# A delta rule followed by a two-layer network: where the rescaling of keys, the masks, the big loads and two steps of the first product stand in the prologue

## The chip, the cores and the metric

The kernel runs on one core of one Trainium2 chip. The metric is the device time of one execution in microseconds (us). The engines are TensorE (PE, matrix products), VectorE (DVE), ScalarE (ACT), GpSimd (POOL) and SyncE (SP, which issues transfers). Each engine takes its instructions in the order of the program, and semaphores hold it until its operands are ready.

## The reference

```python
B, H, S, D = 4, 8, 768, 48
k_n = k / (norm(k) + 1e-6)
state = zeros(B, H, D, D)
for t in range(S):
    y[:, :, t] = einsum('bhd,bhde->bhe', q[:, :, t], state)
    v_old = einsum('bhde,bhd->bhe', state, k_n[:, :, t])
    state += beta[:, :, t] * outer(k_n[:, :, t], v[:, :, t] - v_old)
x = y.transpose(0, 2, 1, 3).reshape(3072, 384)
h = x @ w_in                      # 384 x 2048, given in 64-bit floats
g = h / (1 + exp(-1.702 * h))
out = g @ w_out                   # 2048 x 384, given in 64-bit floats
```

## The kernel before

The sequence of 768 steps is cut into chunks of C = 128, so there are 24 units (6 chunks, 4 batches of 8 heads). Within a chunk the recurrence becomes a triangular system: Gram products of the keys (gram), the inverses of its 32 x 32 diagonal blocks (invert, worked by DVE for 128 blocks at once) and a chain of block solves, called hops (together): PE multiplies, ACT copies the result to SBUF, and the next hop needs the copy. The first four units are whole chunks of one batch each (Step); the later ones are taken as halves (Half). The output of two units forms a tile xT of 256 rows, for which hidden computes gelu(x @ w_in) in 16 steps of two, each of three f32 products of 128 x 256 (ph); the second product is po.

The weights come as 64-bit floats, and DVE turns them into 32-bit floats in six instructions a piece, one of them a clamp on ACT (conversion, line 265). Pieces overlap each other (conversions, 318): the first four are halves of the first two quarters of w_in (128 x 768 words), then six thirds of the other quarters (128 x 512), then the 16 blocks of w_out (128 x 384, two pairs as one). After the first eight blocks the second inverse is worked (invert(1)), then the other eight. All this is one stream called behind. fill(us) (393) records as much of it as us of its own cost estimates, at least one instruction, wherever the program stands; the order on DVE is thus written by hand, by where fill stands and what it is given. A finished piece starts loads of later blocks of raw weights (fetch_in, 236; fetch_out, 253), which go into places that are free by then.

Ahead of the steady part (slot, from unit 3 on, with PE full) stands a prologue:

- keys of units 0 to 3 are loaded, normalized and turned, the first inverse is worked, and the Gram products of these units are made;
- the squares of the keys of units 4 to 7 (the second keys) are summed; roots_second (478) lets POOL take the power, and DVE then rescales the keys;
- the first hops, eight passes of the loop at line 1508 for units 0 and 1. Among them stand warm matmuls (of no use but to keep PE busy), the turning of the second keys by PE (turn, in passes 2 to 5), the masks (select, a POOL instruction of 128 x 1024 for each unit) and the thirds of w_in. paced (1473) lets POOL copy one word of a finished result into the place that a load is to fill, so that the load starts behind that result;
- put_out for units 0 and 1: outputs and states, and ACT copies them to xT;
- the loads of the first three blocks of w_out, of bL (beta for the later inverses, 16 small transfers) and of keys and queries, most of them issued by POOL (other_queue);
- the later hops, the loop at line 1568 for units 2 and 3. Each pass makes a Gram product of the second keys (passes 0 to 2), a step of hidden (feed, 1561) and a fill;
- a loop of 25 passes (1612) with a fill and a feed each, in which the keys of units 8 to 11 are prepared (prepare_early, 1597): ACT squares them, DVE sums, POOL takes the power, DVE adds and inverts (rn), ACT scales the keys in eight instructions, PE turns them (psT), and so on, one step each two passes. Also the scores psQ of unit 4 stand there, in pass 18;
- the first half of po for units 0 and 1 (both_written, 1260), and then slot after slot.

Of the kernel before, what the change touches and what calls it, by code (L numbers as in the profile page):

```python
# [18 lines left out]
def kernel(  # L19
# [28 lines left out]
    KC = DM // 128  # L48
# [3 lines left out]
    HB = 2  # L52
# [84 lines left out]
    def pinned(op):  # L137

        return lambda *a, **kw: tc.keep_in_program_order(op(*a, **kw))  # L139
# [12 lines left out]
    sync, beside = pinned(nc.sync.dma_start), pinned(nc.scalar.dma_start)  # L152
# [30 lines left out]
    def warm(n, after=None):  # L183
        ps = ps_moe.tile([128, 2, 256], F32, tag="moe", name="ps_warm")
        if after is not None:
            after(ps[:, 0, 0:1], 0.0)
        twice = ones.rearrange("p (o k) -> p o k", o=1).broadcast_to([128, 2, 256])
        for _ in range(n // 2):
            pe.matmul(ps, lhsT=ones[:, 0:128], rhs=twice, start=True, stop=True)
        if n % 2:  # L190
            pe.matmul(ps[:, 0], lhsT=ones[:, 0:128], rhs=ones, start=True, stop=True)
# [11 lines left out]
    def as_raw(words, shape):  # L203
        a, b = shape
        return words.rearrange("p (j n o) -> p j n o", j=a, n=b)

    def as_rows(raw):
        return raw.bitcast(moe_w_in.dtype).rearrange("p j n o -> p j (n o)")
# [13 lines left out]
    def quarter(i):  # L222
        size = KC * NQ * 2
        at = 1 if i == 1 else 0
        return as_raw(raws[:, at * size : (at + 1) * size], (KC, NQ))

    def place_thirds():

        for j in range(KC):
            words = g_tile().rearrange("p f t -> p (f t)").bitcast(I32)  # L230
            thirds.append(as_raw(words, (1, NQ)))
        for a in (3072, 2048):
            thirds.append(as_raw(TW[:, a : a + 2 * NQ].bitcast(I32), (1, NQ)))
        thirds.append(as_raw(raws[:, 4 * NQ : 6 * NQ], (1, NQ)))

    def fetch_in(i, other=None, js=None, only=None):

        f = slice(i * NQ, (i + 1) * NQ)
        for j in range(KC) if js is None else js:
            dst = as_rows(thirds[(i - 2) * KC + j])[:, 0] if i >= 2 else as_rows(quarter(i))[:, j]  # L240
            for p, r, m, step in x_rows:
                if only is not None and p // DP != only:
                    continue
                (other if other and (p >= DP or js) else sync)(
                    out=dst[p : p + m], in_=moe_w_in[r + j * step : r + j * step + m, f]
                )
# [6 lines left out]
    def fetch_out(f, dma=sync):  # L253

        if f in outside:
            slot = outside[f]
            if slot not in slots:
                slots[slot] = wk.tile([128, 2 * DM], I32, tag=slot[:2].strip("2"), name="raw", bufs=4 if slot[0] == "M" else 3)
            words = slots[slot]
        else:  # L260
            words = raws[:, inside[f] * DM : (inside[f] + 2) * DM]
        places[f] = as_raw(words, (1, DM))
        dma(out=as_rows(places[f])[:, 0], in_=moe_w_out[f * 128 : (f + 1) * 128, :])
# [129 lines left out]
    def fill(us):  # L393
        while us > 0:
            us -= next(behind, us)
# [82 lines left out]
    def roots_second(areas):  # L478

        z, r = (TW[:, a : a + B * H].rearrange("p (b h) -> p b h", b=B) for a in (1792, 1856))  # L480
        for o in range(2):
            vec.tensor_reduce(z[:, 2 * o : 2 * o + 2], areas[o], axis=AX.X, op=ALU.add)
        pool.tensor_tensor(r, z, half[:, 0:1].broadcast_to([128, B, H]), op=ALU.pow)
        yield
        vec.tensor_scalar(r, r, 1e-6, None, op0=ALU.add)
        vec.reciprocal(r, r)
        for o in range(B):
            K = home(B + o)[:, :, 0:D]
            vec.tensor_tensor(K, K, r[:, o].broadcast_to([128, H, D]), op=ALU.mult)
            if o % HB == 1:  # L490
                yield
# [28 lines left out]
    def gram(n):  # L520

        return gram_whole(n) if n < B else gram_halves(n)
# [267 lines left out]
    def bank(name, shape=(128, H, D), big=False):  # L790
        if late:
            return one_bank(name)[:, 0 : H * D].rearrange("p (h d) -> p h d", h=H)
        from_, tag = (ps_big, "big") if big else (ps_seq, "seq")
        return from_.tile(list(shape), F32, tag=tag, name=name)
# [496 lines left out]
    def run(work):  # L1291
        for _ in work:
            pass
# [13 lines left out]
    def new_step(n):  # L1307
        if n >= len(units):
            return NoStep()
        steps[n] = (Step if n < B else Half)(n)  # L1310
        return steps[n]

    def together(solves, belows):

        solves = [(X, blk) for X, blk in solves if X]
        belows = [(X, blk) for X, blk in belows if X]
        psU = bank("psU") if solves else None
        psRs = [bank("psR") if X.n >= B else None for X, blk in belows]
        for h in range(H):
            for X, blk in solves:  # L1320
                X.solve(blk, h, psU)
            for (X, blk), psR in zip(belows, psRs):
                X.below(blk, h, psR)
        for X, blk in solves:
            X.solved(blk, psU)
        for (X, blk), psR in zip(belows, psRs):
            X.rest(blk, psR)
# [80 lines left out]
    other_queue = pinned(nc.gpsimd.dma_start)  # L1408
# [47 lines left out]
        gram(b)  # L1456
    place_thirds()
    run(invert(0))
    for b in range(HB, B):
        loaded[b] = VU[b]  # L1460
    pair = [new_step(n) for n in range(B)]
# [8 lines left out]
        X.gather()  # L1470
    fine(16)

    def paced(sign, i, j, other=None):

        words = thirds[(i - 2) * KC + j]
        pool.tensor_copy(words[0:1, 0, 0:1, 0].bitcast(F32), sign)
        fetch_in(i, other, js=(j,))

    def hops(a, b):

# [16 lines left out]
    scaling = roots_second(areas)  # L1497
# [1 line left out]
    next(scored)  # L1499
    warm(NM // 2)  # L1500
    next(products)
    for j in range(KC):
        paced(inverse[0][0:1, 0, BS // 2 : BS // 2 + 1], 2, j)
    fill(2.3)
    Nds = []
# [1 line left out]
    merging = merge(pair[2:], area, ((ps_big, "big"), (ps_big, "big")), False)  # L1507
    for i in range(2 * NB):
        together(*next(path))
        if i in (1, 3, 4):  # L1510
            at = pair[i % 2].US[i // 2 * BS : i // 2 * BS + 1, 0:1]
            paced(at, *{1: (3, 0), 3: (3, 1, other_queue), 4: (3, 2, other_queue)}[i])
        if i == 0:
            warm(NM)
            next(products)
            warm(NM // 2)
            next(products)
            run(scored)
        if i == 1:
            for X in pair[:2]:  # L1520
                X.select()
        if i == 2:
            run(scaling)
            for b in range(HB, B):
                load_values(b, sync)
        if 2 <= i <= B + 1:
            turn(B + i - 2)
        if i == B + 2:
            gram(B)
        if i < 2 * NB - 1:  # L1530
            warm(NU if i == 1 else NU // 2)
        fill(2.1)
    put_out(pair[0])
    put_out(pair[1])
    fill(2.0)
# [3 lines left out]
        X.gather()  # L1539
    next(merging)  # L1540
    fill(4.0)
    for at in range(B):
        if at == HB:
            for f in range(3):
                fetch_out(f, other_queue)
        for u in range(2):
            for half_ in range(2):
                lane = at * BS + u * 2 + half_
                other_queue(
                    out=bL[lane : (at + 1) * BS : NB],  # L1550
                    in_=betas[(at % 2 * 2 + u) * H : (at % 2 * 2 + u + 1) * H, 1:, at // 2 * 2 + half_, :],
                )
# [8 lines left out]
    def feed(n=1):  # L1561
        for _ in range(n):
            while ffn and next(ffn[0], None) is None:
                ffn.pop(0)
# [3 lines left out]
    for i in range(2 * NB):  # L1568
        if i == 0:
            feed()  # L1570
            fill(1.5)
            next(merging)
            feed()
            fill(1.5)
            next(merging)
        together(*next(later))
        if i < HB + 1:
            gram(B + 1 + i)
        if 1 <= i <= HB:
            Nds.append(send_blocks(B + i))  # L1580
        if i == HB + 1:
            load_diagonals(Nds + [send_blocks(B + HB + 1)])
        feed()
        fill(2.2)
    for s in pair[2:]:
        put_out(s)
        fill(2.5)
# [22 lines left out]
    starts = {2 * B: 1, 2 * B + 1: 9, 2 * B + 2: 6, 2 * B + 3: 8}  # L1610
    first = new_step(B)
    for i in range(25):
        fill(0.75)
        feed()
        for n, at in starts.items():
            if i >= at and (i - at) % 2 == 0:
                next(early[n], None)
        if i == 8:
            next(first.scored)
            load_queries(B + 1)  # L1620
        if i == 16:
            next(first.scored)
        if i == 18:
            run(first.scored)
# [62 lines left out]
```

## Time and profile before

| | |
|---|---|
| median of three runs | 681.72 us (677.34 to 683.82) |
| the profiled execution | 683.03 us, span 681.3 us |
| PE busy | 662.8 us, 97% of the span |
| DVE busy | 481.8 us, 71% |
| POOL busy | 275.5 us, 40% |
| ACT busy | 233.4 us, 34% |
| mean granted PE clock | 0.990 |

Times in a timeline count from the start of the span. A line gives start, duration, engine, source line, operation, output and inputs, partitions x elements, and in brackets the idle time ahead of the instruction with what ended it. Nearly all instructions pass through one helper, so their source line is 139 and the tiles tell them apart. Busy time of PE comes from modelled ends, so that a slow matmul counts as busy too. "PEclk" is the granted clock of PE in tenths.

### The profile page before, as it was taken

The page shows a single profiled execution, that of the slowest core. Times are in us where ns is not written, and L with a number is a line of the kernel's source. Part 1 is how long each engine was busy: PE and PEld are TensorE (multiplying, and loading weights), DVE is VectorE, ACT ScalarE, POOL GpSimd, SP SyncE. Part 2 cuts the span into 40 slices and gives each one's busy share as a digit, 9 for nine tenths or more (in the row PEclk, how much of TensorE's full clock was granted, in tenths as well). Part 3 has the DMA queues.
Part 4 walks back from the last instruction along what each step waited for, and adds up shares of the span by engine and source line. Part 5 has one row for each costly group of instructions (what it writes and reads, how often), then busy time and mean ns, then how long its engine had stood idle before and what let it go on. Part 6 is the DMA issues. An engine that isn't in the chain of part 4 may idle for free.

```text
span 681.3 us, 21832 instructions
## 1 busy us (share of the span) xinstructions
PE 662.8 (97%) x9334; PEld 569.1 (84%) x9334; DVE 481.8 (71%) x896; ACT 233.4 (34%) x571; POOL 275.5 (40%) x293
## 2 busy tenths in 40 slices
PE   8979989999999999999999999999999999999997
PEld 7756768755678998998998988988988988989997
DVE  6888699996788997996997996997976970200000
ACT  3655554642333233333333233234233233322120
POOL 4043774320286634635535526426305205105041
PEclk9996999999999999999999999999999999999999
DMA  9746567173334435335335244234230130100100
GB/s 164 158 122 122 146 177 176 28 166 84 87 74 91 98 65 107 77 68 106 72 67 116 63 92 89 68 84 80 60 84 13 39 75 1 31 2 5 26 1 23
DMA packets 148672, 54.61 MB, mean 80 GB/s; under 512 B 136800, under 2 KB 141664, under 8 KB 148576
## 3 DMA queue, kind: packets, MB, share of 16 engines
q1 hardware_dynamic: 144928, 45.37, 32.2%
q0 software_dynamic: 3648, 7.86, 4.6%
q8 instruction: 73, 1.20, 0.7%
q14 instruction: 23, 0.19, 0.1%
HBM read 38.37 MB, written 13.63 MB: 76 GB/s over the span
## 4 chain that ended last, share of the span: by engine, by line
PE 76%; DVE 9%; issue 3%; POOL 2%; DMA 2%; ACT 0%; DVEq 0%; POOLq 0%; ACTq 0%
PE po L139 32%; PE ph L139 31%; PE four L139 7%; DVE w_out L139 3%; PE psU L139 2%; PE psR L139 2%; DVE P L139 2%; DMA raw<-in_moe_w_out_dram 1%; DVE YB L139 1%; PE psG L139 1%; DVE NT L139 1%; POOL bL L139 1%; DVE raw L139 1%; DMA w_out<-in_moe_w_out_dram 1%; POOL w_out L139 0%
## 5 line engine op out<-in xcount | busy, mean ns | idle before, releaser
L139 PE MATMUL ph<-xT,w_in 128*128 128x256 f32 x1152 | 260.4, 383 | 1.6 <-ACT TW L139 1.3
L139 PEld LDWEIGHTS ph<-xT,w_in 128*128 128x128 f32 x1152 | 215.2, 190 | 33.0 <-ACT TW L139 2.1
L1142 POOL TENSOR_TENSOR gT<-gT 128x512 f32<-128x512 f32 x80 | 103.0, 1298 | 98.0 <-ACT gT L139 66.0
L139 PE MATMUL po<-w_out,gT 128*128 128x192 f32 (+1 forms) x720 | 138.4, 347 | 0.0
L139 DVE TENSOR_TENSOR P<-NT,YB 64x8 f32<-64x8 f32 (+13 forms) x195 | 124.0, 636 | 5.8
L139 PEld LDWEIGHTS po<-w_out,gT 128*128 128x128 f32 x720 | 118.5, 190 | 11.0 <-ACT o L139 0.5
L139 ACT ACTIVATE gT<-ph 128x512 f32<-128x512 f32 x90 | 53.7, 597 | 153.8 <-PE ph L139 153.8
L139 DVE TENSOR_REDUCE YB<-P 64x4 f32<-64x8 f32 (+13 forms) x195 | 78.4, 402 | 6.7
L139 PE MATMUL po<-TW,gT 128*128 128x192 f32 x480 | 81.8, 328 | 0.0
L139 PEld LDWEIGHTS po<-TW,gT 128*128 128x128 f32 x480 | 78.1, 190 | 0.7
L1008 POOL TENSOR_SCALAR_AFFINE_SELECT M<-M 64x512 f32<-64x512 f32 x40 | 29.8, 745 | 91.1 <-ACT M L139 89.9
L139 DVE TENSOR_TENSOR o<-o,late 128x192 f32<-128x192 f32 x20 | 6.5, 355 | 68.1 <-ACT late L139 67.9
L139 ACT COPY VU<-psU 32x384 f32<-32x384 f32 x96 | 45.0, 469 | 19.6 <-PE psU L139 10.3
L139 DVE TENSOR_TENSOR VU<-VU,psR 32x384 f32<-32x384 f32 x40 | 22.2, 554 | 32.8 <-PE psR L139 32.1
L139 PEld LDWEIGHTS psU<-VU,XBs 32*32 32x32 f32 x1536 | 29.6, 107 | 16.1 <-issue 6.9
L139 DVE TENSOR_TENSOR VU<-VU,four 128x384 f32<-128x384 f32 x19 | 10.4, 549 | 46.0 <-ACT M L139 45.7
L412 POOL TENSOR_TENSOR rn<-ssq,half 128x8 f32<-128x8 f32 x12 | 22.3, 1861 | 50.3 <-DVE ssq L139 50.3
L109 POOL DMA_DIRECT2D KN<-in_k_dram x24 | 17.1, 715 | 59.7 <-PE four L139 45.7
L139 ACT COPY o<-po 128x192 f32<-128x192 f32 (+1 forms) x44 | 14.6, 333 | 74.8 <-PE po L139 72.7
L139 PE MATMUL psU<-VU,XBs 32*32 32x48 f32 x1536 | 35.0, 206 | 1.9 <-ACT VU L139 1.5
L139 DVE TENSOR_TENSOR P<-NT 64x512 f32<-64x512 f32 (+7 forms) x45 | 30.5, 678 | 1.1
L139 DVE TENSOR_REDUCE NT<-P 64x32 f32<-64x512 f32 (+9 forms) x45 | 30.0, 668 | 1.6
(168 smaller groups left out, 768.0 us busy)
## 6 DMA issues: line engine op xcount, KB each, us to landing
VU<-in_v_dram SPq DMA_DIRECT2D x40, 96.0 KB, 3.0
out_dram<-o SPq DMA_DIRECT2D x40, 96.0 KB, 2.4
QW<-in_q_dram SPq DMA_DIRECT2D x76, 48.0 KB, 2.2
Kd<-KN SPq DMA_DIRECT2D x56, 64.0 KB, 2.2
late<-Kd SPq DMA_DIRECT2D x14, 256.0 KB, 2.8
KN<-in_k_dram POOLq DMA_DIRECT2D x32, 96.0 KB, 3.1
w_out<-in_moe_w_out_dram SPq DMA_DIRECT2D x7, 384.0 KB, 4.4
NT<-Nd SPq DMA_DIRECT2D x20, 128.0 KB, 2.6
```

The source lines that it names most:

```text
L109: dma(out=place(dst, n)[rows, :, 0:D], in_=src[b, :, t, :].rearrange("h p d -> p h d"),)
L139: return lambda *a, **kw: tc.keep_in_program_order(op(*a, **kw))
L412: nc.gpsimd.tensor_tensor(rn, ssq, half, op=ALU.pow)
L1008: nc.gpsimd.affine_select(out=M, in_=M, compare_op=ALU.is_gt, fill=0.0, base=0, pattern=[[0, H], [1, CH]], channel_multiplier=-1,)
L1142: (engine or nc.gpsimd).tensor_tensor(o, a, b, op=op)
```

## The change

The second keys are rescaled in pass 1 of the first hops instead of pass 2, and pass 0 records 0.5 us of conversions ahead of its warm matmuls and 1.5 behind instead of 2.1 behind. The masks of units 0 and 1 are applied in pass 4 instead of pass 1. The first third of the third quarter of w_in is loaded right behind the first inverse, without a pacing copy. Two thirds of the last quarter, and the first three blocks of w_out, are issued by SP instead of POOL, the blocks ahead of the bL loads. In passes 0 to 2 of the later hops two steps of hidden are made and 3.4 us of conversions recorded, instead of one step and 2.2. The loop of 25 passes records 0.55 us each instead of 0.75, and makes a step of hidden in two of three passes.

```diff
     place_thirds()
     run(invert(0))
+    fetch_in(2, js=(0,))
...
-    def paced(sign, i, j, other=None):
+    def paced(sign, i, j):
 
         words = thirds[(i - 2) * KC + j]
         pool.tensor_copy(words[0:1, 0, 0:1, 0].bitcast(F32), sign)
-        fetch_in(i, other, js=(j,))
+        fetch_in(i, js=(j,))
...
-    for j in range(KC):
+    for j in range(1, KC):
         paced(inverse[0][0:1, 0, BS // 2 : BS // 2 + 1], 2, j)
     fill(2.3)
...
     for i in range(2 * NB):
         together(*next(path))
+        if i == 4:
+            for X in pair[:2]:
+                X.select()
         if i in (1, 3, 4):
             at = pair[i % 2].US[i // 2 * BS : i // 2 * BS + 1, 0:1]
-            paced(at, *{1: (3, 0), 3: (3, 1, other_queue), 4: (3, 2, other_queue)}[i])
+            paced(at, *{1: (3, 0), 3: (3, 1), 4: (3, 2)}[i])
         if i == 0:
+            fill(0.5)
             warm(NM)
             next(products)
             warm(NM // 2)
             next(products)
             run(scored)
         if i == 1:
-            for X in pair[:2]:
-                X.select()
+            run(scaling)
         if i == 2:
-            run(scaling)
             for b in range(HB, B):
                 load_values(b, sync)
...
             warm(NU if i == 1 else NU // 2)
-        fill(2.1)
+        fill(2.1 if i else 1.5)
     put_out(pair[0])
     put_out(pair[1])
...
     fill(4.0)
+    for f in range(3):
+        fetch_out(f, sync)
     for at in range(B):
-        if at == HB:
-            for f in range(3):
-                fetch_out(f, other_queue)
         for u in range(2):
...
             load_diagonals(Nds + [send_blocks(B + HB + 1)])
-        feed()
-        fill(2.2)
+        feed(2 if i < HB + 1 else 1)
+        fill(3.4 if i < HB + 1 else 2.2)
...
     for i in range(25):
-        fill(0.75)
-        feed()
+        fill(0.55)
+        if i % 3 < 2:
+            feed()
```

## The prediction

> **What bounds the kernel now.** I read the page's slices first, then busy time by stretch, then the waits of VectorE (DVE), then the timelines of the engines between 40 and 160 us.
>
> ```profile
> span 681.3 us, 21832 instructions
> ...
> PEclk9996999999999999999999999999999999999999
> ```
>
> ```profile
> 48.00:50.00 2.00, 0.15 (x2) 0.18 (x3) 1.93 (x5) 0.30 (x1) 0.13 (x1) 1.00 0.76 205
> ...
> 52.00:64.00 12.00, 12.00 (x172) 8.13 (x166) 10.20 (x15) 5.95 (x11) 5.89 (x10) 0.50 0.80 157
> ...
> 124.00:141.00 17.00, 14.48 (x124) 11.31 (x122) 16.42 (x31) 11.54 (x39) 6.63 (x5) 1.00 0.27 47
> ...
> 160.00:200.00 40.00, 40.00 (x724) 25.64 (x722) 26.75 (x57) 11.84 (x31) 16.31 (x19) 1.00 0.37 83
> ```
>
> The columns are the stretch, its length, busy time of PE, weight loads, DVE, ACT and POOL, then clock and DMA. From 160 us on PE is busy all the time, and both kernels issue the same matmuls, so the change can only move the moment at which PE gets there. Before that DVE is the fullest engine (16.42 of 17 us). The one slice of low clock follows a pause of PE at 48 us, and lasts to 64.
>
> ```profile
> DVE w_out L139 <- DMA raw<-in_moe_w_out_dram: 5.7, 2, 4.6
> DVE w_in L139 <- ACT w_in L139: 5.7, 5, 1.6
> ```
>
> ```profile
> 46.04 2.65 DVE L139 TENSOR_SCALAR w_out<-w_out 128x768 int32<-128x768 int32 x1
> 48.61 0.16 DVE L139 TENSOR_SCALAR TW<-TW 128x32 f32<-128x32 f32 x1
> ...
> 82.44 0.36 DVE L139 TENSOR_SCALAR w_out<-raw 128x384 int32<-128x384 int32 x1 [4.64 <-DMA raw<-in_moe_w_out_dram]
> ...
> 108.20 1.22 DVE L139 TENSOR_TENSOR NT<-NT,bL 128x1024 f32<-128x1024 f32 x1
> ...
> 133.96 0.16 DVE L139 TENSOR_SCALAR rn<-rn 128x8 f32<-128x8 f32 x1
> ```
>
> ```profile
> 37.69 5.52 POOL L139 TENSOR_TENSOR TW<-TW,half 128x32 f32<-128x32 f32 x1 [19.53 <-DVE TW L139]
> ...
> 46.00 2.14 POOL L139 TENSOR_SCALAR_AFFINE_SELECT M<-M 128x1024 f32<-128x1024 f32 x2
> ...
> 77.22 1.77 POOL L139 DMA_DIRECT2D raw<-in_moe_w_out_dram  x3
> ```
>
> ```profile
> 49.85 0.63 PE L139 MATMUL psT<-ident,KN 128*128 128x128 f32 x4 [2.46 <-issue]
> ...
> 124.56 0.60 PE L139 MATMUL psT<-ident,KN 128*128 128x128 f32 x4
> ...
> 137.52 1.00 PE L139 MATMUL psQ<-QS,kT 48*64 48x112 f32 x32 [0.65 <-ACT QS L139]
> ...
> 141.81 10.59 PE L139 MATMUL po<-w_out,gT 128*128 128x384 f32 x32
> ```
>
> The mask's affine_select on POOL holds a DVE instruction from 46.04 to 48.69; the same shape at 40.13 takes 0.69. Behind it waits the rescaling (48.61), and behind that PE's transpose of the second keys (2.46 us idle). At 82.44 DVE has waited 4.64 us for the first block of w_out, whose load POOL issued at 77.22, after eight loads of bL.
>
> **The change, part by part.** I follow DVE's lead, that is how much sooner it starts the same instruction, up to the start of the second inverse (108.20, call it S), and then what hangs on DVE.
>
> *Rescaling and clamp.* The new fill(0.5) puts the second clamp on ACT ahead of the merge copies, so DVE's wait of 1.63 us at 45.05 goes. The rescaling now stands right behind the first piece (ends 42.8) and waits for POOL's power (37.69 + 5.52 = 43.21): it starts at 43.3, takes 2.46 (48.61 to 51.07), and the three conversions it overtook take 0.66 + 0.98 + 0.62 = 2.2. The instruction that began at 51.07 begins at 47.9: lead 3.2. PE's transpose finds its keys at 44.5, and its 2.46 us go.
>
> *Masks later.* The two selects keep their 2.14 us; behind POOL's copy of the third hop they start near 51.6, where DVE has no idle time, so the 2.0 us come back: lead 1.2. Nothing waits for the masks before the outputs at 66.
>
> *The clock.* The 12 us at 0.50 follow the pause of PE. Without the pause I expect full clock there. The hops' ACT copies now start at 53.10, 56.85, 60.60, 64.35, 3.75 us apart; at full clock a hop takes 0.93 to the first copy (0.90 from 44.29 and 0.96 from 46.50), 1.6 for two copies and kT and 0.41 to the next hop, 2.95 in all. Then the clamps that DVE waits for (1.60 at 62.84, 0.86 at 66.52, 1.16 at 71.18) come in time: lead 1.2 + 3.6 = 4.8, and the hops end some 4.8 sooner. If the light hop work lets the clock fall all the same, only the earlier start of 2.1 us is left.
>
> *Loads by SyncE.* Six big loads leave POOL for SP. In the hops SP idles from 53.6 to 70.17, so eight issues of 0.5 us there hide in that pause. The first third, issued near 35, falls into 35 to 44 us, where the DMA share is under 0.3: cost nothing. The three w_out blocks follow xT and Nd on SP: these took 70.17 to 75.46, so from 65.4 they end at 70.7. To landing the trace has 2.9 to 5.9 us, median 4.4 for SP; with little else in flight I take 3.7, so 74.4. DVE gets there at 77.79 - 4.8 = 73.0 and waits 1.4 instead of 4.64: lead 8.0 (5.3 if the clock stays low, by the same steps; at most 10.8, the sum of DVE's waits from 40 to 108). POOL's sixteen bL loads end sooner than now. On SP the blocks 9 and 10, which wait for DVE, now stand ahead of the last Nd and the four NT loads, for which the second inverse waits: by rows of 2.4 (Nd), 7.1 (NT) and 2.4 to 5.9 to landing this costs S between nothing and 3.6 us. I take nothing, since 3.4 of the 7.1 were waits for Nd that run out sooner.
>
> *Two steps of x @ w_in in three later hops.* Nine more f32 products go there, and leave the 25-step loop. Each is two rows of 0.219 us (17.10 / 78), 9 x 0.438 = 3.94 us of PE. They fill PE's waits for ACT's copies there. PE follows DVE out of these hops, since the copy of the last hop stands behind a clamp that needs DVE: PE enters the loop near 103 instead of 107.6.
>
> *What this does to the loop.* This is the step I weigh most. Each fill of the loop emits at least one product of the inverse (over 1 us), whether it asks for 0.75 or 0.55, so DVE's order keeps the start it got from fill(3.4): in the changed order the roots of the first keys that the loop prepares (KN0, unit 8) stand behind the 768-product, four products later, and those of the last keys behind the whole inverse.
>
> ```profile
> 121.22 1.91 ACT L139 ACTIVATE KN<-KN,rn 128x48 f32<-128x48 f32 x8 [1.05 <-DVE rn L139]
> ...
> 135.16 1.90 ACT L139 ACTIVATE KN<-KN,rn 128x48 f32<-128x48 f32 x8
> 136.96 0.51 ACT L139 ACTIVATE QS<-ST 128x384 f32<-128x384 f32 x1
> ```
>
> ACT scales the keys with these roots, and PE's transposes and psQ wait for ACT. Counted from S: the first roots now end at 12.9 and will at 19.0; with ACT's 1.9 PE's transpose can start at S + 21.1. From 103 PE has 27 products ahead of it (39 now), 27 x 0.438 = 11.8 us, so it stands there at 114.9 and waits to 121.3 (S at 100.2), some 6 us. The last roots move from S + 26.2 to S + 32.0 (the 768, 448 and 512 products, 1.93 + 1.31 + 1.45, and NT, 1.14). ACT then still owes other keys, a clamp and a gelu (to S + 33.4), scales for 1.9 and copies QS for 0.5: psQ at S + 36.1, now S + 29.3. That is 6.8 later, and PE idles some 7 us before it. Behind psQ stand nine products that stood ahead of it: po follows psQ by 7.2 instead of 4.3 us. So po comes 6.8 + 2.9 = 9.7 us later after S than now.
>
> *The clock once more.* Waits of 6 and 7 us are longer than the 2.46 that halved the clock. The slow work in the first gap is hidden by the second. Behind psQ the cost lies between 0 (no drop) and 6.5 us (13 us at half clock, as from 51 to 64). Dense 128x128 products should bring it back sooner than small hop tiles; I take 2.2. The Trainium skill (TensorE: Matmul & The Clock Gate, Part 1: The HAM clock gate) says that one idle window of about 3.4 us halves the clock and one busy window restores it: by that 3.4 us at half clock, and the estimate would be 1.7 in place of 2.2. Our trace agrees that a pause comes first, but its 12 us are longer than one window.
>
> *The end.* The 0.96 us that PE idles between 155 and 160, behind ACT's clamp of the last block, go, since DVE is ahead of PE there: -1.0 (or 0).
>
> Sum: -8.0 + 9.7 + 2.2 - 1.0 = +2.9 us. The profiled execution took 683.03 us (span 681.3), so 685.9; against the median of 681.72 that is 684.6.
>
> **The rivals.** *The gain is kept.* If PE does not wait for the roots, because DVE leads by more or the loop's order bites less than I read it, DVE's conversions set the end and the lead of 8.0 is the gain: 673.7. For it speaks that DVE waits for only 1.5 us (0.49 and 1.05) between 85 and 158, so that each us of lead stays; against it the changed order itself.
>
> *The cold clock decides.* If PE's activity in the hops is too low and the clock falls there as now, the lead is 5.3; and if the waits of 6 and 7 us then bring 13 us at half clock on po, the sum is -5.3 + 9.7 - 1.0 + 6.5 = +9.9: 691.6. It decides from the point where the second wait holds long enough for a drop, some 2.5 us. For it speaks that PE, counted busy, stayed at 0.50 for 12 us; against it that the clock was 1.00 in all denser stretches.
>
> *SP is the bound.* NT lands late by the full 3.6 us: 684.6 + 3.6 = 688.2. The trace shows SP's NT loads waiting for Nd, but 3 us of room before S.
>
> *It does not do what it says.* The rescaling stays tied to POOL's power; were that 5 us later, the transpose would wait again and the lead at 51 would be gone: about 688. Nothing moves the power, so little chance.
>
> **How the numbers follow.** Forecast 0.60, gain kept 0.14, cold clock 0.20, SP or the power 0.06. A measurement of this kernel tells about 1%, 6.8 us, from no change: faster than 674.9 is nearly all of the gain kept, 0.13; slower than 688.5 is the cold clock and a part of the forecast's upper end, 0.23; within 0.64. The forecast's own range is 679.6 (lead 10.8, no clock cost: -2.1) to 689; the range for 8 in 10 is 676 to 691.
>
> **What would show it.** Right: PE's transpose of the second keys without a wait and full clock from 50 to 64; the first w_out block within 2 us; S near 100; then PE idle about 6 us ahead of psT and 7 ahead of psQ in the loop, po near 146 (141.81 - 8.0 + 9.7 + 2.2), 143.5 if the clock holds. Wrong: po before 138, or PE busy through the loop (then the gain is kept), or S later than 105.

## The result and the profile after

The changed kernel takes 685.44 us (median of 14 runs), the kernel before 681.76 us in the same series (median of 14): ratio 1.0084, 95% interval 1.0057 to 1.0111. The ratios leave out runs more than 1.5% above the fastest of the same kernel, which the medians contain, so that the medians alone give 1.0054. So the change makes the kernel slower by a little, less than the 1% from which the prediction spoke of a difference. The forecast was 684.6 us. The profiled execution took 688.01 us, its span 686.1 (before: 683.03 and 681.3).

The page's head and clock slices, and busy time by stretch (columns as in the prediction: length, busy PE, weight loads, DVE, ACT, POOL, then clock and DMA share):

```profile
span 686.1 us, 21826 instructions
...
PEclk9989989889999999999999999999999999999999
```

```profile
52.00:64.00 12.00, 11.44 (x274) 7.91 (x262) 9.53 (x15) 9.99 (x20) 3.10 (x4) 1.00 0.66 137
124.00:141.00 17.00, 9.96 (x95) 7.98 (x94) 13.19 (x29) 10.69 (x36) 7.03 (x6) 0.78 0.51 111
...
160.00:200.00 40.00, 40.00 (x629) 25.19 (x631) 21.39 (x48) 10.67 (x27) 11.45 (x15) 1.00 0.30 70
```

The one deep slice of low clock (52 to 64 us) has become three shallow dips: by stretches of 1 us, 0.50 from about 45 to 51, 99 to 106 and 133 to 143 us. In the loop PE, which was busy for 14.48 of 17 us at full clock, is now busy for 9.96 at 0.78; from 160 us on it is full as before. The timelines of DVE, of SP's queue, and of PE:

```profile
43.42 0.18 DVE L139 TENSOR_SCALAR TW<-TW 128x32 f32<-128x32 f32 x1 [0.24 <-POOL TW L139]
...
75.55 0.36 DVE L139 TENSOR_SCALAR w_out<-raw 128x384 int32<-128x384 int32 x1 [1.27 <-DMA raw<-in_moe_w_out_dram]
...
102.07 1.22 DVE L139 TENSOR_TENSOR NT<-NT,bL 128x1024 f32<-128x1024 f32 x1
...
133.04 0.16 DVE L139 TENSOR_SCALAR rn<-rn 128x8 f32<-128x8 f32 x1
```

```profile
71.24 2.58 SPq L139 DMA_DIRECT2D raw<-in_moe_w_out_dram  x3
...
94.40 2.12 SPq L139 DMA_DIRECT2D NT<-Nd  x4
```

```profile
42.31 0.60 PE L139 MATMUL ps_warm<-ident 128*128 128x512 bf16 x2 [1.13 <-issue]
...
97.77 0.23 PE L139 MATMUL psU<-VU,XBs 32*32 32x48 f32 x1 [2.93 <-ACT VU L139]
...
109.98 12.22 PE L139 MATMUL ph<-xT,w_in 128*128 128x256 f32 x54
122.04 0.91 PE L139 MATMUL psT<-ident,KN 128*128 128x128 f32 x4
...
137.28 1.77 PE L139 MATMUL psQ<-QS,kT 48*64 48x112 f32 x32 [7.04 <-ACT QS L139]
138.99 2.93 PE L139 MATMUL ph<-xT,w_in 128*128 128x256 f32 x6
...
147.82 10.79 PE L139 MATMUL po<-w_out,gT 128*128 128x384 f32 x32
```

The rescaling starts at 43.42 instead of 48.61. DVE waits 1.27 us for the first block of w_out instead of 4.64. The second inverse starts at S = 102.07, 6.1 us sooner than the 108.20 of before. But the last roots end at S + 31.4 instead of S + 26.2, PE waits 7.04 us before psQ, and po begins at 147.82, 6.0 us later than before.

So the span falls into three parts, which can be compared across kernels: S; from S to po; and from po to the end. Before they were 108.20 + 33.61 + 539.5; now they are 102.07 + 45.75 + 538.3. The lead gives 6.1 back, the loop takes 12.1, the end gives 1.2: +4.8, which is the difference of the spans.

All kernels that ran, with the three parts of their profiled executions. Each ratio is against runs of the kernel before in the same series; its medians there were 681.76 us (changed), 683.91 (e1 to e4), 682.41 (e5 to e8) and 682.14 (e10 to e13), so ratios of different series are comparable to some tenths of a percent only:

| kernel | median us | ratio to before, 95% interval | S | S to po | po to end |
|---|---|---|---|---|---|
| before | 681.76 | | 108.20 | 33.61 | 539.5 |
| changed | 685.44 | 1.0084, 1.0057 to 1.0111 | 102.07 | 45.75 | 538.3 |
| e1, without the loop part | 674.85 | 0.9872, 0.9824 to 0.9920 | 99.55 | 33.71 | 539.2 |
| e2, loop part alone | 697.44 | 1.0188, 1.0132 to 1.0245 | 112.83 | 44.86 | 538.4 |
| e3, changed + products ahead of psQ | 686.78 | 1.0036, 1.0000 to 1.0071 | 100.25 | 47.60 | 538.3 |
| e4, changed, short fills | 679.61 | 0.9984, 0.9948 to 1.0021 | 102.11 | 37.61 | 538.2 |
| e5, e1 with long fills | 678.67 | 0.9961, 0.9928 to 0.9993 | 100.61 | 39.00 | 538.0 |
| e6, loads alone | 683.75 | 0.9999, 0.9961 to 1.0037 | 103.88 | 33.56 | 539.2 |
| e7, rescaling, clamp, masks alone | 675.74 | 0.9902, 0.9865 to 0.9939 | 99.68 | 33.53 | 539.3 |
| e8, e4 with psQ earlier | 678.93 | 0.9957, 0.9922 to 0.9991 | 102.36 | 36.32 | 538.2 |
| e10, e3 in a free bank | 683.89 | 1.0059, 1.0028 to 1.0091 | 104.79 | 44.31 | 538.2 |
| e11, masks alone | 677.24 | 0.9939, 0.9910 to 0.9967 | 102.56 | 33.60 | 539.2 |
| e12, rescaling and clamp alone | 675.72 | 0.9917, 0.9885 to 0.9949 | 104.79 | 33.40 | 539.6 |
| e13, before + products in the hops | 679.44 | 0.9968, 0.9937 to 0.9998 | 102.15 | 33.62 | 539.9 |

Whatever has the old loop needs 33.4 to 33.7 us from S to po. S itself varies from one execution to the next with the clock in the hops, so a single S is weak evidence, and the ratios decide there.

### The profile page after: what moved, and what is told of

It is laid out like the page before. It is cut to its first block, busy times and chain, and to the rows that moved or that the text cites. A ratio compares the mean times of both kernels' runs of the same rounds, so it can differ in the third digit from the quotient of the medians.

```text
span 686.1 us, 21826 instructions
## 1 busy us (share of the span) xinstructions
PE 665.6 (97%) x9334; PEld 571.3 (83%) x9334; DVE 479.8 (70%) x896; ACT 234.0 (34%) x571; POOL 268.8 (39%) x281
## 3 DMA queue, kind: packets, MB, share of 16 engines
q1 hardware_dynamic: 145744, 47.60, 33.1%
## 4 chain that ended last, share of the span: by engine, by line
PE 90%; DVE 5%; ACT 2%; DMA 1%; issue 1%; POOL 0%; DVEq 0%; POOLq 0%; ACTq 0%
PE ph L139 34%; PE po L139 34%; PE four L139 7%; PE psU L139 3%; PE ps_warm L139 3%; PE psR L139 2%; PE psG L139 2%; DVE P L139 2%; PE psQ L139 1%; DVE YB L139 1%; DVE w_out L139 1%; PE psT L139 1%; DVE NT L139 1%; ACT VU L139 1%; PE psZ L139 1%
## 5 line engine op out<-in xcount | busy, mean ns | idle before, releaser
L139 PE MATMUL ph<-xT,w_in 128*128 128x256 f32 x1152 | 264.5, 387 | 0.6 <-DMA xT<-last 0.5
L139 PEld LDWEIGHTS ph<-xT,w_in 128*128 128x128 f32 x1152 | 217.6, 192 | 32.5 <-DMA xT<-last 0.9
```

## The experiments: the loop

**e1, the rest without the loop part.**

```diff
-        feed(2 if i < HB + 1 else 1)
-        fill(3.4 if i < HB + 1 else 2.2)
+        feed()
+        fill(2.2)
...
-        fill(0.55)
-        if i % 3 < 2:
-            feed()
+        fill(0.75)
+        feed()
```

> The changed kernel with the two edits on x @ w_in and Gram products put back: one step and fill(2.2) in every later hop, fill(0.75) and a step in every pass of the 25-pass loop. Theory A (the loop pays: these edits put the last roots behind the inverse, PE waits 7.0 us before psQ, its clock halves there, and that eats the lead of 6.1 us that DVE has at S = 102.1): PE's wait before psQ falls under 1.5 us, no clock drop between 132 and 144, DVE keeps 5 to 6.5 us of lead up to 160, ratio to before 0.990 to 0.993 (some 675.5 us). Rival B (the rest of the change is no gain: the lead at S is lost again behind other waits, as that for the last w_out block at 156, or the cold stretch at 44 to 51 costs it): ratio 0.997 to 1.003. Rival C (the cost sits in the rest, as in SP's loads): ratio over 1.003.

PE's timeline around psQ:

```profile
128.97 1.00 PE L139 MATMUL psQ<-QS,kT 48*64 48x112 f32 x32 [0.65 <-ACT QS L139]
...
133.26 10.59 PE L139 MATMUL po<-w_out,gT 128*128 128x384 f32 x32
```

674.85 us, ratio 0.9872 (0.9824 to 0.9920). psQ comes at S + 29.4, where the kernel before has S + 29.3, with a wait of 0.65, and the clock is 1.00 from 74 us on (0.50 from about 67 to 74). The median is 10.6 us below the changed kernel's. Theory A holds, with somewhat more gain than it said (ratio under its range, po 8.6 us sooner than before instead of 5 to 6.5); B and C fall. This kernel has the lowest median of all, and beats both kernels; e7 and e12 lie within 1 us of it.

**e2, the loop part alone.** The reverse of e1's edit, in the kernel before.

> The kernel before with only the two edits on x @ w_in and Gram products: two steps and fill(3.4) in the first three later hops, fill(0.55) and steps in two of three passes of the loop. Theory A: S stays within 1 us of 108.2 less what the longer fills give, PE waits 5 to 8 us before psQ and the clock halves there, po comes 9 to 13 us after its 141.8, ratio to before 1.012 to 1.018. Rival B (the edits cost little by themselves, PE has slack there): ratio 0.998 to 1.005.

```profile
148.05 1.77 PE L139 MATMUL psQ<-QS,kT 48*64 48x112 f32 x32 [5.92 <-ACT QS L139]
```

697.44 us, ratio 1.0188 (1.0132 to 1.0245), slightly over the range of theory A. S to po is 44.86, and PE waits 5.92 us before psQ. po comes 15.9 us later than before, where 9 to 13 were expected, because S came at 112.83: in this execution the half clock of the hops lasted from 50 to 74 us, and DVE waited 4.97 us for a clamp at 75.4. That part stands ahead of the edit. In the later hops PE waits 4.54 us for ACT's copies (108.52), and the clock is at 0.50 from there to 118.

**e4, short fills in the later hops.** DVE's order of roots and inverse changes, PE's order does not.

```diff
         feed(2 if i < HB + 1 else 1)
-        fill(3.4 if i < HB + 1 else 2.2)
+        fill(2.2)
```

> The changed kernel with fill(2.2) for fill(3.4) in the first three later hops; the second step of x @ w_in stays there, and the loop stays as changed. PE's order is that of the changed kernel, only DVE's order differs: the first roots of the loop stand ahead of the 392-product and the last ones ahead of the 768-product again. Theory A' (it is DVE's order, not PE's, that makes PE wait): the wait of 7.0 before psQ falls under 2.5 us, the clock drops there less or not, po comes 7 to 10 us sooner, ratio to before 0.990 to 0.995. Rival (it is the move of the nine products: PE reaches psQ early whatever DVE does, and nine products stand behind psQ): PE still waits over 4 us before psQ and the ratio is 1.002 or more.

```profile
130.64 1.77 PE L139 MATMUL psQ<-QS,kT 48*64 48x112 f32 x32 [6.26 <-ACT QS L139]
...
139.72 10.79 PE L139 MATMUL po<-w_out,gT 128*128 128x384 f32 x32
```

Neither theory got it whole. psQ is back at S + 28.5, and po comes 8.1 us sooner, as A' has it. But PE still waits 6.26 us, as the rival has it: with nine products fewer ahead of it, it only comes early. po then follows psQ by 9.1 us (4.3 in e1), since the nine products stand behind psQ and the clock has halved. The ratio, 0.9984 (0.9948 to 1.0021), lies between the two.

**e5, long fills without the moved products.**

```diff
         feed()
-        fill(2.2)
+        fill(3.4 if i < HB + 1 else 2.2)
```

> The kernel of e1 with fill(3.4) for fill(2.2) in the first three later hops: one step of x @ w_in per hop, and the loop, as in the kernel before. With e1, e4 and the changed kernel it closes a square of two edits (longer fills; the moved products). Theory A' (two prices that add: the longer fills put the last roots behind the inverse and cost some 6 us, as e4 against the changed kernel; the moved products cost some 5, as e4 against e1): roots end at S + 31, psQ near S + 35, PE waits 3 to 6 us before psQ, po follows psQ by 4.3 to 6 us, 680 to 682.5 us, ratio to before 0.994 to 0.999. Rival (the longer fill does harm only because PE, with nine products fewer ahead, comes early): ratio 0.987 to 0.991. Rival (the fill is the whole cost): ratio over 1.003.

```profile
135.32 1.00 PE L139 MATMUL psQ<-QS,kT 48*64 48x112 f32 x32 [0.65 <-ACT QS L139]
...
139.61 10.59 PE L139 MATMUL po<-w_out,gT 128*128 128x384 f32 x32
```

psQ at S + 34.7, as expected, and po 4.3 behind it. The waits expected before psQ came to less, 0.48 + 0.90 + 0.65; as I read it, because products were left to work off. 678.67 us, under the range; the ratio, 0.9961 (0.9928 to 0.9993), is within it. With this the square is closed, in S to po: neither 33.7 (e1), long fills 39.0 (+5.3), moved products 37.6 (+3.9), both 45.75 (+12.0). So in these executions the two edits cost some 3 us more together than one by one. As I read it, the moved products are the cover that PE would have had while the roots are late. The times of the runs bear this out only weakly: against e1 the medians rise by 3.8, 4.8 and 10.6 us, which leaves 2.0 for the two together, and the ratios leave less than 1 us, within their intervals.

**e8, QS and psQ earlier in e4's loop.**

```diff
-        if i == 16:
+        if i == 12:
             next(first.scored)
-        if i == 18:
+        if i == 13:
             run(first.scored)
```

> The kernel of e4 with QS and psQ taken at passes 12 and 13 of the loop instead of 16 and 18, so that ACT copies QS ahead of two scalings of keys. If PE waits before psQ because QS stands behind the keys in ACT's queue, that wait falls under 1.5 us, the clock does not drop there, po comes 3 to 5 us sooner than e4's 139.7, and DVE's conversions take over as the bound: 676 to 678 us, ratio to before 0.990 to 0.994. Rival (the nine products are missing wherever PE waits for the keys: the wait moves to the transpose of the last keys): a wait of 4 us or more there, ratio 0.996 or more.

```profile
125.20 1.77 PE L139 MATMUL psQ<-QS,kT 48*64 48x112 f32 x32 [4.70 <-ACT QS L139]
...
138.68 10.79 PE L139 MATMUL po<-w_out,gT 128*128 128x384 f32 x32
```

Ahead of psQ PE waits 4.70 us instead of 6.26, and po comes 1.3 us sooner after S. QS still stands behind one scaling of keys on ACT (122.82 to 124.73), which needs the roots that DVE ends at 122.8, behind the 768-product. So the first expectation fails: ACT's queue is a small part, and DVE's order sets this. The rival did not come as said either: a wait of over 4 us is there, but still ahead of psQ and not at the transpose. 678.93 us, ratio 0.9957 (0.9922 to 0.9991), between the two ranges and not told apart from e4.

**e3 and e10, filling PE's wait before psQ.** In e3 `warm(44)` at pass 18, that is 22 bf16 products; in e10 the same products in another PSUM pool:

```diff
         if i == 18:
+            ps = ps_acc.tile([128, 2, 256], F32, tag="acc", name="ps_free")
+            twice = ones.rearrange("p (o k) -> p o k", o=1).broadcast_to([128, 2, 256])
+            for _ in range(22):
+                pe.matmul(ps, lhsT=ones[:, 0:128], rhs=twice, start=True, stop=True)
             run(first.scored)
```

> The changed kernel with 22 bf16 products 128x512 ahead of psQ, at pass 18 of the loop, which fill 5 to 6.5 us of PE's wait of 7.0; nothing else differs. If the clock that halves behind this wait costs what I read from the trace (ph x6 in 2.93 for 1.56, psQ 1.77 for 1.00, psT 1.06 for 0.60, po 10.5 us behind psQ), the clock stays at 1.00 from 132 to 146 and po comes 3.0 to 3.6 us sooner: ratio to before 1.003 to 1.005, some 3.3 us below the changed kernel. If the cold stretch is hidden (DVE or ACT set po's start), it stays at 1.008. If the cold clock is the whole of the loss, as a third theory has it, the ratio falls under 0.999.

```profile
133.25 7.20 PE L139 MATMUL ps_warm<-ident 128*128 128x512 bf16 x22 [4.83 <-ACT TW L139]
```

e3 answered another question. Its products took the PSUM tile (a place for results of PE) that ACT had still to empty, waited 4.83 us for it, ran at half clock until about 138 us, and pushed psQ to S + 40.1. What followed psQ then ran at full clock: po 7.5 us behind it, where 7.2 was reckoned. S to po became longer, 47.60 instead of 45.75, so that the ratio, 1.0036 (1.0000 to 1.0071), lies in the expected range for another reason than the expected one.

> e3 again with the 22 filling products in a PSUM bank that nothing else holds at that time (in e3 they took one that ACT had still to empty, and so began 4.8 us late). If the clock behind PE's wait costs what I read from the trace, it stays at 1.00 from 134 to 146, psQ starts as in the changed kernel, counted from S, and po follows it by 7.2 us instead of 10.5: 3.0 to 3.6 us less than the changed kernel's 685.4, ratio to before 1.002 to 1.005. If the cold stretch is hidden, 1.007 or more; if it is the whole loss, under 0.999.

PE's timeline of e10, and its busy time by stretch:

```profile
132.80 4.91 PE L139 MATMUL ps_free<-ident 128*128 128x512 bf16 x22
140.00 1.66 PE L139 MATMUL psQ<-QS,kT 48*64 48x112 f32 x32 [2.29 <-ACT QS L139]
```

```profile
140.00:142.00 2.00, 2.00 (x33) 1.72 (x34) 0.00 (x0) 0.74 (x3) 0.00 (x0) 0.54 0.86 232
```

Here the products begin at once, but are 2.29 us short, and behind that the clock halves, for some 3.5 us instead of 10. po follows psQ by 9.1 us instead of 10.5 and S to po falls by 1.4. 683.89 us, ratio 1.0059 (1.0028 to 1.0091), just outside the range; it overlaps with that of the changed kernel. psQ still comes at S + 35.2, 5.9 us later than before, though the clock was at 1.00 from 79 to 140 us. So the cold clock is a part of the loss and not the whole. The full 3.0 to 3.6 us that I put on it was not tested, since the pause was not filled to its end.

## The experiments: the lead

**e6, the loads alone.** The six loads as in the change, the rest as before.

> The kernel before with only the six big loads moved to SyncE's queue (the first third already behind the first inverse). By my steps the wait of 4.64 us before the first w_out block falls to 1.5 to 2.5, since SP issues the block right behind xT and Nd while DVE comes no sooner; S comes 2 to 3 us sooner, ratio to before 0.995 to 0.998. Rival (SP is the bound: the blocks stand ahead of Nd and the NT loads, for which the second inverse waits): NT lands late, ratio 1.000 or more.

```profile
88.28 0.36 DVE L139 TENSOR_SCALAR w_out<-w_out 128x384 int32<-128x384 int32 x1 [2.12 <-DMA w_out<-in_moe_w_out_dram]
```

Ratio 0.9999 (0.9961 to 1.0037): no gain is seen, though the interval allows up to 0.4%. DVE's wait for the first block of w_out is gone altogether, but it now waits 2.12 us for a later one. The profiled execution took 678.33 us, well below the median of 683.75, and had cold stretches from 44 to 51 and 72 to 78 us instead of 50 to 64, so its S of 103.88 does not speak for the loads. In it the issue of the NT loads began at 90.78 and took 4.36 us, and DVE did not wait for them. So the rival has the ratio that it named, but not by its reason: SP is not the bound.

**e7, rescaling, clamp and masks alone; e12, the same with the masks left at pass 1; e11, the masks alone.** Their edit is the change's own:

```diff
+        if i == 4:
+            for X in pair[:2]:
+                X.select()
...
         if i == 0:
+            fill(0.5)
...
         if i == 1:
-            for X in pair[:2]:
-                X.select()
-        if i == 2:
             run(scaling)
...
-        fill(2.1)
+        fill(2.1 if i else 1.5)
```

> The kernel before with only the rescaling a hop sooner, fill(0.5) ahead of the merge and the masks later. By my steps PE's pause of 2.46 us and the cold stretch from 50 to 64 go, DVE is 3 to 5 us ahead at the end of the hops. If POOL, which follows the hops, issues w_out's blocks sooner by as much, the lead stays: S 3.5 to 5 us sooner, ratio to before 0.991 to 0.995. Rival (the load is late then: the wait at the first w_out block grows by what the hops gain, and only both edits together pay): wait over 7 us, ratio 0.998 or more.

```profile
69.28 1.85 POOL L139 DMA_DIRECT2D raw<-in_moe_w_out_dram  x3
```

```profile
74.45 0.36 DVE L139 TENSOR_SCALAR w_out<-raw 128x384 int32<-128x384 int32 x1 [2.14 <-DMA raw<-in_moe_w_out_dram]
```

e7: 675.74 us, ratio 0.9902 (0.9865 to 0.9939), clock 1.00 throughout, and S at 99.68, 8.5 us sooner, more than the 3.5 to 5 expected. POOL, which still issues w_out's first blocks, does so at 69.28 instead of 77.22; DVE waits 2.14 us for them. So the load follows the hops by itself. Against e1, which has the loads too, the median of e7 is 0.9 us higher, and the runs of both (673.89 to 676.64, 674.24 to 677.49) overlap. In e1 the first block comes in time, but DVE waits for a later one:

```profile
84.08 0.36 DVE L139 TENSOR_SCALAR w_out<-w_out 128x384 int32<-128x384 int32 x1 [2.00 <-DMA w_out<-in_moe_w_out_dram]
```

> The kernel of e7 with the masks left at hop 1: only the rescaling and the clamp sooner. By my steps the lead of the rescaling (3.2 us) and the clock need nothing of the masks, whose 2.0 us are paid in the one place or in the other: ratio to before 0.988 to 0.994, within 2 us of e7. Rival (the masks carry the gain): ratio 0.997 or more.

e12: 675.72 us, ratio 0.9917 (0.9885 to 0.9949), the median of e7 to 0.02 us. No difference is seen from where the masks stand, once the rescaling is early. Its profiled execution took 679.54 us, its slowest, with stretches at 0.50 around 65 to 68, 79 to 81 and 93 to 99 us, which go with the late S.

> The kernel before with only the two masks moved from hop 1 to hop 4. POOL no longer holds DVE at 46 us, so the rescaling starts 2.0 us sooner and PE's pause before the second keys shrinks from 2.46 to about 0.5. If the pause is what halves the clock, it stays at 1.00 from 50 to 64 and S comes 2 to 4 us sooner: ratio to before 0.992 to 0.997. Rival (the masks only move their 2.0 us to another place): 0.998 to 1.002.

e11: ratio 0.9939 (0.9910 to 0.9967). The rescaling starts at 46.70, PE's pause shrinks from 2.46 to 0.51 us, and the clock stays at 1.00. So each of the two ways out of the pause, earlier rescaling (e12) and later masks (e11), does most of the work, and together (e7) they add little.

**e13, the pause filled with nothing but products.**

```diff
+        if i == 2:
+            warm(18)
         if 2 <= i <= B + 1:
             turn(B + i - 2)
```

> The kernel before with nine bf16 products 128x512 ahead of the first transpose of the second keys, which fill most of PE's pause of 2.46 us there; nothing else differs, DVE's order and masks are those of before. If the clock alone makes the lead in the hops, it stays at 1.00 from 50 to 64, and S comes 3 to 5 us sooner: ratio to before 0.992 to 0.996. Rival (DVE's own order makes the lead, the clock is hidden beside it): 0.999 or more.

PE's timeline, and the stretch that ran at 0.50 before:

```profile
47.43 2.12 PE L139 MATMUL ps_warm<-ident 128*128 128x512 bf16 x9
49.96 0.63 PE L139 MATMUL psT<-ident,KN 128*128 128x128 f32 x4 [0.41 <-issue]
```

```profile
52.00:64.00 12.00, 11.44 (x259) 8.54 (x260) 11.76 (x18) 9.84 (x22) 4.59 (x10) 1.00 0.85 158
```

```profile
76.31 0.36 DVE L139 TENSOR_SCALAR w_out<-raw 128x384 int32<-128x384 int32 x1 [2.35 <-DMA raw<-in_moe_w_out_dram]
```

DVE's rescaling stands where it stood (48.72), only PE no longer idles, and the clock stays at 1.00. S moves to 102.15. With e11 this shows that the cold stretch from 50 us on needs the pause. It does not show that the pause always brings it. The ratio is 0.9968 (0.9937 to 0.9998), just outside the range: less than the 6 us of S, because the kernel before does not always have that stretch. In the series of e10 to e13 its times include 676.84 us at a mean granted clock of 0.999 and 686.54 at 0.984, while e13 has 677.46 to 680.71. With the clock alone, DVE's wait for the first block of w_out also falls, from 4.64 to 2.35 us, though POOL still issues it.

## Why the prediction was right

The sum was +2.9 us; the medians differ by 3.7, the spans of the profiled executions by 4.8. The mechanism came about mostly as written: DVE's lead is won, the loop takes more than that back, through late roots, missing products and the clock. One term, the loads, was mis-sized and one wait came elsewhere. That 684.6 lies within 1 us of the median is in part luck: the lead missed by 1.9 us in the profiled execution, and the kernel before has medians from 681.76 to 683.91 in different series.

*Rescaling.* Right. The instruction of 51.07 begins at 48.09, a lead of 3.0 (3.2 forecast), and PE finds its keys without a wait.

*Masks.* Right in sum: they lengthen DVE's work by about 1.8 us at 46.36 in e12 and by 1.7 at 53.27 in e7. In the changed kernel POOL's two selects come at 55.18 and fall mostly into a wait of 2.30 us that DVE has there for ACT.

*Clock in the hops.* Right that the stretch needs the pause (e13), and 52 to 64 us ran at 1.00. The waits for clamps of 1.60, 0.86 and 1.16 us are gone in e13, as forecast. But the profiled execution has a half-clock stretch from about 45 to 51 us instead, behind a pause of 1.13 us at 42.31, and a lead at S of 6.1. e3, which is the same code up to there, kept 1.00 until 69 us (then 0.50 from about 70 to 73 and 97 to 100) and has S at 100.25: a lead of 7.95, where 8.0 was forecast.

*Loads.* The term that was mis-sized. It took 3.2 us of the lead (4.64 less 1.4). Alone they gave no gain that is clear of noise (e6), and on top of the rescaling 0.9 us by the medians, 2 by the ratios, with overlapping intervals (e7 against e1). I set DVE 4.8 us earlier against a load that stayed where it was, but POOL's queue moves with the hops too (77.22 to 69.28 in e7). The wait of 4.64 us falls to 2.35 with the clock alone (e13) and to 2.14 with the rescaling (e7). With SP's loads it is 1.27 in the changed kernel and nothing in e1 and e6, but in these two it moves to a later block (2.00 and 2.12). So the rest of the lead that I gave to the loads belongs to the rescaling and the clock, since e7 reaches 8.5 without them.

That the early load of the first third costs nothing was not borne out either. With the loads, the DMA share from 35 to 38 us is 0.91 to 1.04 instead of 0.45 to 0.67. Seven of the eight kernels that have them show a pause of PE of 0.43 to 1.25 us ahead of the warm matmuls at about 41 us; e1 does not, nor does any of the six without them. In three of the seven (changed, e6, e10) the clock is then at 0.50 for 7 to 10 us. What links the load to the pause the traces do not show.

*The loop.* Forecast +9.7 and +2.2 for the clock, 11.9; S to po grew by 12.1. Within it the roots cost less (psQ at S + 35.2 for 36.1) and what follows psQ more (10.5 us for 7.2 + 2.2): the half clock lasts until about 143 us, 6 us past psQ, and against the 7.5 us of e3 it costs some 3.0. The two errors nearly cancel, which is luck.

*The first wait.* Wrong. PE was to enter the loop near 103 and idle some 6 us before psT; it entered at 109.98 and did not wait. The wait moved into the later hops:

```profile
95.79 0.94 ACT L139 ACTIVATE w_out<-w_out,low 128x768 int32<-128x768 int32 x1 [2.61 <-DVE w_out L139]
```

With fill(3.4) this clamp stands behind more of DVE's work, ACT's copies of the hop stand behind the clamp, and PE waits 2.93 us for them (97.77); then the clock is at 0.50 from about 99 to 106. In e4, with the short fills, PE enters 0.7 us after S, in the changed kernel 7.9 us after it. As I read it, this cost next to nothing, since the roots set psQ in any case: they end at S + 31.4 in e5 too, where PE waits only 1.15 us at this place (96.31), and psQ comes at S + 34.7 there.

*The end.* -1.0 forecast, 539.5 to 538.3 measured. It goes with a late po and not with an early DVE alone: the kernels with S to po over 36 us have 538.0 to 538.4, all others 539.2 to 539.9, e1 and e7 with their lead of over 8 us among them.

*The rivals.* *The cold clock decides* came true in part: half clock in the hops at another place, with a lead of 6.1 between its 5.3 and the forecast's 8.0, and some 3.0 us behind psQ instead of its 6.5. *SP is the bound* fell: NT's loads were issued from 94.40 on, and DVE starts the inverse without a wait. *It does not do what it says* fell: POOL's power ended at 43.39, and the rescaling began at 43.42. *The gain is kept* had the right figure for a kernel that was not this one: 673.7 forecast, 674.85 for e1, where the loop is left alone.

## What to carry to other kernels

Cut the span at a point where one engine takes over (here S and po): if a part takes the same time in every kernel that shares its code (here 33.4 to 33.7 us), the run-to-run scatter of the other parts no longer hides what an edit does to it. Before work is moved out of a loop to fill another engine's waits elsewhere, ask who sets the loop's last operand; if it is not the engine that does the work, the moved work was the cover of that wait. And a lead is not the sum of the waits that it removes: a load issued by a queue that follows the same work comes sooner by itself, and a wait that is removed can come back at the next block.

## What the runs showed of the hardware

The clock halves behind pauses of PE, but their length alone does not tell whether it does. Between 30 and 160 us, every pause of 2.29 us or more in these profiled executions went with a clock of 0.50: 2.46 (before), 2.29 ahead of psQ (e10), 2.93 and 7.04 (changed). Pauses from about 1 to 2.3 us went either way: 1.13 at 42.31 in the changed kernel and 2.09 at 95.94 in e3 were followed by 0.50; 1.25 at 41.94 in e3, 1.92 at 79.24 in e7 and 2.26 at 123.98 in e10 were not. Even behind 0.43 us, at 41.18 in e10, the clock was at 0.50 until 51 us, while 0.41 (e13) and 0.51 (e11) were not followed by it. The Trainium skill (TensorE: Matmul & The Clock Gate, Part 1: The HAM clock gate) has a free-running window of about 3.4 us: an idle one halves the clock, a busy one restores it. The some 3.5 us at half clock in e10 agree with the way back; the pauses of 2.29 and 2.46 us are shorter than that window, and there the measurement decides. Once halved, the clock stayed so for about 4.7 us of dense products in e3 and some 6 us of mostly dense products behind psQ in the changed kernel. In the hops, with their small tiles, it stayed so for about 7 us in the changed kernel, 13.6 before and 24 in e2; what sets this length no run here shows.
